# Strassen's seven products for the last 512 tokens of the second feed-forward layer, with its operand sums on GpSimd

## The chip, the cores and the metric

The kernel runs on one core of one Trainium2 chip. The time is the device time of one run in microseconds (us). The core has a matrix engine (TensorE, PE in the profile; PEld is its loading of weights), VectorE (DVE), ScalarE (ACT), GpSimd (POOL), and SyncE (SP), which issues the DMAs here. Each engine takes its instructions in program order and waits on semaphores for the others.

## The reference, cut to what matters

```python
x = attention(q, k, v)                     # 1536 tokens x 512
x = moe(x)                                 # first feed-forward layer, 512 -> 1024 -> 512
h = x @ w_in2                              # 512 -> 2048
g = np.where(h > 0, h, np.exp(np.minimum(h, 0)) - 1)
out = g @ w_out2                           # 2048 -> 512, the product that is changed for 512 of the 1536 tokens
```

Everything is in float32. A product of two float32 matrices is made here of three fast ones: each operand is split in a rounded part `hi` and the rest `lo`, and `mm3x` adds hi·hi, hi·lo and lo·hi in PSUM (lines 104 to 107).

## The kernel before

The 1536 tokens are three blocks of 512 (`TC`). The second layer has 16 slices of 128 features (`KF2`). Block 0 goes slice by slice. Blocks 1 and 2 make their first product `h` together, over eight pairs of slices (`NP3`, the loop over `p` at the end, 14.95 us a pair), with seven products of 512 columns in place of eight. In the same loop block 1's second product is done for the features that are ready (`fill`), and block 2's `g` is kept for later: `elu` makes g, splits it at once (ACT writes hi, DVE writes lo) into `g2[p]`. After the loop come two last fills of block 1, and then the **last stage**: block 2's second product, 16 slices x 4 token tiles x 3 matmuls = 192 matmuls of 512 columns, with g (128x128) as the weights and `w_out2`'s slice (512 columns) as the moving operand. The slices of `w_out2` lie split in DRAM (`w4d`) and are read back by `load_w4`, into three slots in turn (`w4r[n % 3]`) in the loop, and into larger space in the last stage.

PE's order in this part is the order of the code (`manual_schedule`). The order on ACT, DVE, POOL and SP is set by the scheduler, within the dependences; each engine then runs its list strictly in order. POOL has no work after 280 us. VectorE's instruction for lo is `lo_of` (line 102): a tensor_tensor that reads both inputs from SBUF.

Of the kernel before, what the change touches and what calls it, by code (L numbers as in the profile page):

```python
# [52 lines left out]
def tile_kernel(ctx: ExitStack, tc: tile.TileContext, qd, kT, v, w_in, w_out, g_ln, w_in2, w_out2,  # L53
                ident_d, mask_d, avg_d, out):
    nc = tc.nc
    scale = 1.0 / math.sqrt(D)
# [450 lines left out]
    for t, (j, n) in enumerate(ticks):  # L507
# [92 lines left out]
    def store(i, ops, t):  # L600
        o = rows[t]
        r0 = i * TC + t * 128
        if i == NTOK // TC - 1 and t == NTT - 1:
            for c in range(2):
                cs = slice(c * 256, (c + 1) * 256)
                if c:
                    nc.vector.tensor_copy(o[:, cs], ops[t][:, cs])
                else:
                    nc.scalar.activation(o[:, cs], ops[t][:, cs], AF.Copy)
                nc.sync.dma_start(out[r0:r0 + 128, cs], o[:, cs])  # L610
            return
# [54 lines left out]
    for p in range(NP3):  # L666
        w, c11, c12, c21 = w3_hl[p], *(psb.tile([128, TC], F32, tag="b", name=x) for x in ("c11", "c12", "c21"))
        s1, s2, s7, c22 = small
        product(c11, w["A11"], yf["B11"], True)
# [22 lines left out]
        if p + 2 < NP3:
            sums_w3(p + 2)
        if p:
            load_w4(KF2 + 2 * p + 1)
            if p + 1 == NP3:
                w4l_t = p_w3.tile([128, 6, 2, TC], F32R, tag="last", name="w4l")
                w4l[:] = [w4l_t[:, c] for c in range(6)]
                for n in range(2 * KF2, 2 * KF2 + 6):
                    load_w4(n)  # L700
# [5 lines left out]
        g2[p] = pool.tile([128, 2, 2, TC], F32R, tag=tag, name="g2", **({"bufs": 2} if p < 2 else {}))  # L706
# [71 lines left out]
```

## Time and profile before

| | us |
|---|---|
| median of 3 runs | 487.21 (486.96 to 487.42) |
| the profiled execution | 487.4 |
| its span, first to last instruction | 485.6 |
| PE busy | 460.9 (95%) |
| DVE, ACT, POOL busy | 331.9, 283.9, 127.4 |
| last stage (192 matmuls) | 437.98 to 481.50 |

The page divides the span in 40 slices of 12.1 us and gives the busy tenths of each engine. A timeline row gives start, duration, engine, line and operation, `out<-in` by the program's names, the shape, and in brackets the idle time ahead of it with what ended it. A matmul's shown duration holds its pipeline's latency, so the pace is read from start to start.

### The profile page before, as it was taken

To read this page: it belongs to the slowest core of one execution; us is meant where nothing else is said; L and a number is where in the kernel's file an instruction comes from. 1 tells how busy PE (TensorE), PEld (TensorE's weight loads), DVE (VectorE), ACT (ScalarE), POOL (GpSimd) and SP (SyncE) were. 2 spreads that over 40 slices of the span, in tenths; PEclk is the share of its full clock that TensorE was granted. 3 is DMA by queue.
4 is the path that set the end of the run, shared out by engine and by line. 5 is a ranking of instruction groups with operands and counts; after the bars stand their busy time and mean duration, and the time that the engine had idled before them with its cause. 6 is when DMAs were issued, how large, how long until landed. Compare 5 with 4: busy or idle time off the path is not lost.

```text
span 485.6 us, 7410 instructions
## 1 busy us (share of the span) xinstructions
PE 460.9 (95%) x2568; PEld 390.8 (80%) x2568; DVE 331.9 (68%) x747; ACT 283.9 (58%) x623; POOL 127.4 (26%) x200
## 2 busy tenths in 40 slices
PE   0989999899999999999999999999999999999996
PEld 0566787789997998899888888888888888888885
DVE  3698968997679377969997999557675565550000
ACT  1776777885658347655954757457676666660001
POOL 2798467476434222312232200000000000000000
PEclk9989999899999999999999999999999999999999
DMA  8993997254163413397579663651212212378112
GB/s 287 353 361 126 303 268 231 83 189 122 59 182 115 156 59 102 107 331 266 199 249 317 248 208 132 205 186 43 79 52 88 86 45 87 104 301 289 45 43 86
DMA packets 40117, 82.47 MB, mean 170 GB/s; under 512 B 9616, under 2 KB 18448, under 8 KB 40080
## 3 DMA queue, kind: packets, MB, share of 16 engines
q1 hardware_dynamic: 40080, 82.00, 51.0%
q8 instruction: 20, 0.33, 0.3%
q14 instruction: 17, 0.14, 0.1%
HBM read 70.46 MB, written 11.53 MB: 169 GB/s over the span
## 4 chain that ended last, share of the span: by engine, by line
PE 80%; DVE 12%; POOL 2%; issue 2%; ACT 2%; DMA 1%; SPq 0%; POOLq 0%; DVEq 0%
PE o_ps L107 9%; PE o_ps L105 9%; PE o_ps L106 9%; PE h L107 6%; PE h L105 6%; PE h L106 6%; PE c L107 5%; PE c L105 5%; PE c L106 5%; PE y_ps L105 4%; PE y_ps L107 4%; PE y_ps L106 4%; PE s_ps L216 3%; DVE conv L128 2%; DVE sm L222 2%
## 5 line engine op out<-in xcount | busy, mean ns | idle before, releaser
L126 POOL TENSOR_SCALAR conv<-conv 128x512 f32<-128x512 f32 x48 | 40.1, 838 | 91.1 <-ACT conv L123 87.1
L230 POOL TENSOR_SCALAR sm<-sm,st 128x120 f32<-128x120 f32 x96 | 49.4, 532 | 21.6 <-ACT ln L279 8.5
L105 PE MATMUL o_ps<-w4r,g_hl 128*128 128x512 f32 x128 | 49.8, 389 | 0.0
L106 PE MATMUL o_ps<-w4r,g_hl 128*128 128x512 f32 x128 | 49.8, 389 | 0.0
L107 PE MATMUL o_ps<-w4r,g_hl 128*128 128x512 f32 x128 | 45.3, 390 | 0.0
L105 PE MATMUL y_ps<-lnT,w_out 128*128 128x384 f32 x128 | 43.6, 341 | 1.0 <-DVE lnT L102 1.0
L105 PE MATMUL h<-w_in,xT 128*128 128x512 f32 x96 | 40.6, 423 | 3.3 <-ACT xT L136 3.3
L106 PE MATMUL y_ps<-lnT,w_out 128*128 128x384 f32 x128 | 43.2, 337 | 0.0
L107 PE MATMUL y_ps<-lnT,w_out 128*128 128x384 f32 x128 | 42.9, 337 | 0.0
L225 ACT ACTIVATE sm<-sm,st 128x120 f32<-128x120 f32 x96 | 36.8, 389 | 5.9 <-DVE st L222 5.9
L216 PE MATMUL s_ps<-kw,q_bd 128*128 128x120 f32 x192 | 28.5, 298 | 11.7 <-POOL kw L98 11.4
L107 PE MATMUL h<-w_in,xT 128*128 128x512 f32 x96 | 39.1, 407 | 0.2 <-DVE xT L102 0.2
L106 PE MATMUL h<-w_in,xT 128*128 128x512 f32 x96 | 38.7, 403 | 0.0
L216 PEld LDWEIGHTS s_ps<-kw,q_bd 128*128 128x128 f32 x192 | 26.8, 211 | 13.0 <-POOL kw L98 11.4
L613 DVE COPY y<-o_ps 128x512 f32<-128x512 f32 x5 | 3.5, 690 | 42.9 <-PE o_ps L107 42.9
L585 ACT ACTIVATE y<-y 128x512 f32<-128x512 f32 x48 | 30.0, 628 | 0.8
L127 DVE TENSOR_SCALAR conv<-conv 128x512 int32<-128x512 int32 x48 | 24.1, 503 | 8.7 <-POOL conv L126 8.7
L615 ACT ACTIVATE y<-o_ps 128x512 f32<-128x512 f32 x6 | 3.6, 599 | 43.9 <-PE o_ps L107 43.9
L106 PEld LDWEIGHTS o_ps<-w4r,g_hl 128*128 128x128 f32 x128 | 24.1, 188 | 5.1
L107 PEld LDWEIGHTS o_ps<-w4r,g_hl 128*128 128x128 f32 x128 | 23.9, 188 | 5.2 <-DVE g_hl L102 0.2
L105 PEld LDWEIGHTS o_ps<-w4r,g_hl 128*128 128x128 f32 x128 | 24.0, 188 | 4.9
L123 ACT ACTIVATE conv<-y 128x512 f32<-128x512 f32 x30 | 20.1, 671 | 13.5 <-DMA y<-in_w_in 11.9
(146 smaller groups left out, 1259.7 us busy)
## 6 DMA issues: line engine op xcount, KB each, us to landing
w4r<-w4d SPq DMA_DIRECT2D x38, 512.0 KB, 3.5
y<-in_w_in SPq DMA_DIRECT2D x16, 512.0 KB, 5.3
w4d<-w3f SPq DMA_DIRECT2D x16, 512.0 KB, 3.0
y<-in_w_out SPq DMA_DIRECT2D x14, 512.0 KB, 5.8
q_bd<-in_qd SPq DMA_DIRECT2D x24, 256.0 KB, 6.6
bits<-in_w_out SPq DMA_DIRECT2D x10, 512.0 KB, 4.8
w4l<-w4d SPq DMA_DIRECT2D x10, 512.0 KB, 4.2
vw<-in_v SPq DMA_DIRECT2D x24, 192.0 KB, 5.8
```

Of the source, the lines that this page charges most:

```text
L105: nc.tensor.matmul(ps, lhsT=l[0][ls], rhs=r[0][rs], start=first, stop=False, skip_group_check=parts)
L106: nc.tensor.matmul(ps, lhsT=l[0][ls], rhs=r[1][rs], start=False, stop=False, skip_group_check=parts)
L107: nc.tensor.matmul(ps, lhsT=l[1][ls], rhs=r[0][rs], start=False, stop=last, skip_group_check=parts)
L123: first = nc.scalar.activation(x, high.bitcast(F32), AF.Abs)
L126: nc.gpsimd.tensor_scalar(x, x, F64_HUGE, F64_TINY, op0=ALU.min, op1=ALU.max)
L127: nc.vector.tensor_scalar(a, a, 3, 0x3FFFFFF8, op0=ALU.logical_shift_left, op1=ALU.bitwise_and)
L128: nc.vector.scalar_tensor_tensor(a, high, -0x40000000, a, op0=ALU.bitwise_and, op1=ALU.bitwise_or)
L216: nc.tensor.matmul(sps[:, p, 0:KW], lhsT=q_bd[n][:, p, :], rhs=kw[:, p, :], start=True, stop=True)
L222: nc.vector.tensor_tensor_reduce(sm[:, p, :], sps[:, p, 0:KW], mask[:, mi, :], -scale, 3.0e38, op0=ALU.add, op1=ALU.min, accum_out=nm[:, p ...
L225: nc.scalar.activation(sm[:, p, :], sm[:, p, :], AF.Exp, bias=nm[:, p:p + 1], scale=-1.0, accum_out=ss[:, p:p + 1])
L230: nc.gpsimd.tensor_scalar(sm[:, p, :], sm[:, p, :], ri[:, p:p + 1], 1.0, op0=ALU.mult, op1=ALU.mult)
L585: nc.scalar.activation(m, m, AF.Exp, scale=-1.0)
```

## The change

**Second product of block 2.** For each pair `p` of slices, g is seen as 2x2 quarters (two slices by two halves of 256 tokens) and w_out2 as 2x2 quarters (two slices by two halves of 256 columns). `half` makes one of Strassen's seven products for it, of two token tiles with 256 columns: 6 matmuls, and so 8 x 7 x 6 = 336 matmuls of 256 columns in place of 192 of 512. The seven sums stay in seven PSUM banks over all pairs and are put together at the end, on DVE (`result`). Pairs 0 to 5 run pair by pair; the last two run product by product, so that the results come out one after the other.

**Operands.** Strassen's sums of w_out2's quarters (`sums_w4`, per pair two adds of 512 columns, which put hi and lo together again, and four of 256) and of g's quarters (`sums_g`, four of 256) are tensor_tensor instructions on POOL. `elu_m` now leaves g unsplit in `g2[p]`. `parts_g(p)` splits three pieces late, each with one copy on ACT and one `lo_of` on DVE: three quarters of g (768 columns), the sums of w_out2 (1024) and the sums of g (1024). `sums_g` of pairs 0, 1, 2, 4 and 6 write the same space in turn (`raw`), of pairs 3, 5 and 7 another. `load_b` brings the three quarters of w_out2 that are used as they are.

```diff
     def place_w4(n):
-        n -= 2 * KF2
-        return w4r[n % 3] if n < 0 else w4l[n % 6] if n < 10 else wt[:, (3, 4, 1, 2, 0, 3)[n - 10]]
+        return w4r[n % 3]
...
+    def elu_m(h2, m):
+        nc.scalar.activation(m, h2, AF.Relu, scale=-1.0)
+        nc.scalar.activation(m, m, AF.Exp, scale=-1.0)
+        nc.vector.scalar_tensor_tensor(m, m, -1.0, h2, op0=ALU.add, op1=ALU.max)
...
+    def add(out_, a, b, op=ALU.add):
+        nc.gpsimd.tensor_tensor(out_, a, b, op=op)
+
+    def sums_w4(p):
+        x = g2[0][:, 2048:3072].rearrange("p (c f) -> p c f", c=2)
+        t = g2[p][:, 1024:2048].rearrange("p (s f) -> p s f", s=4)
+        for c in range(2):
+            hi, lo = w4_hl[KF2 + 2 * p + c]
+            add(x[:, c], hi.bitcast(F32), lo.bitcast(F32))
...
+        add(t[:, 0], b12, b11, ALU.subtract)
+        add(t[:, 1], b22, t[:, 0], ALU.subtract)
+        add(t[:, 2], b22, b12, ALU.subtract)
+        add(t[:, 3], b21, t[:, 1], ALU.subtract)
...
+    def raw(p):
+        return g2[0 if p > 1 and p % 2 else 1][:, 2048:3072].rearrange("p (s f) -> p s f", s=4)
+
+    def sums_g(p):
...
+        add(sl[:, 0], a21, a22)
+        add(sl[:, 1], sl[:, 0], a11, ALU.subtract)
+        add(sl[:, 2], a11, a21, ALU.subtract)
+        add(sl[:, 3], a12, sl[:, 1], ALU.subtract)
+
+    def parts_g(p):
+        m = g2[p][:, 0:1024].rearrange("p (s f) -> p s f", s=4)
+        a, su, tu = last["a"][p % 3], unit(2 * p), unit(2 * p + 1)
+        for t, x in ((a, m[:, 0:3]), (tu, g2[p][:, 1024:2048].rearrange("p (s f) -> p s f", s=4)), (su, raw(p))):
+            first = nc.scalar.activation(t[:, 0], x, AF.Copy)
+            if p:
+                tc.keep_in_program_order(first)
+            lo_of(t[:, 1], x, t[:, 0])
+
+    def half(p, x, ps):
...
+        for t in range(2):
+            mm3x(ps[:, t], l, (al, slice(t * 128, (t + 1) * 128)), r, (al,), p == 0 and t == 0, p == NP3 - 1, True)
...
         for c, h2 in ((1, c22), (0, c12)):
-            ghl[2 * KF2 + 2 * p + c] = [g2[p][:, c, i] for i in range(2)]
-            elu(h2, ghl[2 * KF2 + 2 * p + c])
+            elu_m(h2, g2[p][:, (1 - c) * TC:(2 - c) * TC])
+        sums_w4(p)
...
-    ops = tiles_o()
-    for f in range(KF2):
-        for t in range(NTT):
-            ffn2_out(ops, t, 2 * KF2 + f)
-            if f == KF2 - 1:
-                store(2, ops, t)
-        if f != 9:
-            load_w4(2 * KF2 + f + 6 - (f > 9))
+    parts_g(1)
+    sums_g(2)
...
+    order = (1, 6, 7, 5, 2, 3, 4)
...
+    for p in range(NP3 - 2):
+        parts_g(p + 2)
+        if p + 3 < NP3:
+            sums_g(p + 3)
+        for x in order:
+            half(p, x, acc[x])
+        load_b(p + 3)
+    u1, u2, u3, u4 = tmp
+    for x in order:
+        for p in range(NP3 - 2, NP3):
+            half(p, x, acc[x])
+        if x == 1:
+            nc.scalar.activation(u1, acc[1], AF.Copy)
+        elif x == 6:
+            nc.vector.tensor_tensor(u2, acc[6], u1, op=ALU.add)
...
+        else:
+            result(4, u3, res[3], 1, 0)
```

How the change moves instructions is shown at three places. Brackets give what an instruction waits for; `Pool`, `DVE`, `Activation` and `PE` are the engines, `DMAHW` are DMAs.

GpSimd, the end of its list. Before, it ends with conversions of weights at 280 us:

```order
L126 TENSOR_SCALAR conv_85<-conv_85 128x512 [waits DVE_49,Activation_49]
L126 TENSOR_SCALAR conv_85<-conv_85 128x512 [waits Activation_49] x6
L126 TENSOR_SCALAR conv_85<-conv_85 128x512 [waits Activation_49]
L774 UNCONDITIONAL_BRANCH
L774 ISA [waits barrier_Pool_Activation_PE_DVE_SP_gather]
```

Now, around the start of the last stage (`g2_3298` is g2[0], `g2_3406` g2[1], `g2_3514` g2[2], `g2_3622` g2[3], `g2_3730` g2[4], `g2_4065` g2[7]):

```order
L648 TENSOR_TENSOR g2_3298<-w4r_2424 128x512 [waits DMAHW5_49]
L648 TENSOR_TENSOR g2_4065<-g2_3298,g2_4065 128x256 [waits Pool_49]
L648 TENSOR_TENSOR g2_4065<-g2_3298 128x256
L648 TENSOR_TENSOR g2_3298<-g2_3298,g2_3622 128x256 [waits Pool_49]
L648 TENSOR_TENSOR g2_3298<-g2_3622 128x256 [waits Pool_49]
L648 TENSOR_TENSOR g2_3298<-g2_3622,g2_3298 128x256 [waits Pool_49]
L648 TENSOR_TENSOR g2_3406<-g2_3514 128x256 [waits DVE_49]
L648 TENSOR_TENSOR g2_3406<-g2_3406,g2_3514 128x256 [waits Pool_49]
L648 TENSOR_TENSOR g2_3406<-g2_3514,g2_3406 128x256 [waits Pool_49]
L648 TENSOR_TENSOR g2_3406<-g2_3730 128x256 [waits DVE_49]
```

The rest of `sums_w4(7)` and of `sums_g(3)` stand ahead of `sums_g(2)` (the row `g2_3406<-g2_3514`), whose first add waits for DVE's last split of pair 1; `sums_g(4)` waits likewise for pair 2. Sixteen more adds follow `sums_g(2)`: pairs 4, 5, 6 and 7.

VectorE, the end of its list. Before, it has only the end of the loop and copies of results:

```order
L586 SCALAR_TENSOR_TENSOR y2_67<-y2_67,c12_3942 128x512 [waits Activation_49]
L102 TENSOR_TENSOR g_hl_2423<-y1_66,g_hl_2423 128x512 [waits Activation_49]
L102 TENSOR_TENSOR g2_4035<-y2_67,g2_4035 128x512 [waits Activation_49]
L613 COPY y0_65<-o_ps_3252 128x512 [waits DMAHW1_49,PE_49]
L613 COPY y0_65<-o_ps_3254 128x512 [waits DMAHW3_49,PE_49]
L613 COPY y0_65<-o_ps_4079 128x512 [waits DMAHW3_49,DVE_49,PE_49]
L607 COPY y0_65<-o_ps_4081 128x256 [waits DMAHW6_49,Activation_49]
```

Now (`s4` are slots for split sums):

```order
L606 COPY y0_65<-o_ps_3252 128x512 [waits DMAHW7_49,PE_49]
L606 COPY y0_65<-o_ps_3254 128x512 [waits DMAHW1_49,PE_49]
L102 TENSOR_TENSOR w4l_4017<-g2_3406,w4l_4017 128x768 [waits Activation_49]
L102 TENSOR_TENSOR s4_4025<-g2_3406,s4_4025 128x1024 [waits Activation_49]
L102 TENSOR_TENSOR s4_4024<-g2_3406,s4_4024 128x1024 [waits Activation_49]
L102 TENSOR_TENSOR w3e_3198<-g2_3514,w3e_3198 128x768 [waits Activation_49]
L102 TENSOR_TENSOR s4_4090<-g2_3514,s4_4090 128x1024 [waits Activation_49]
L102 TENSOR_TENSOR g_hl_2423<-g2_3406,g_hl_2423 128x1024 [waits Activation_49]
L102 TENSOR_TENSOR w3e_2096<-g2_3622,w3e_2096 128x768 [waits PE_49,Activation_49]
```

The splits of pairs 1 to 7, 21 `lo_of` in all, three a pair, stand behind the copies of block 1's last results (line 606).

ScalarE in the loop's first pair (`c11`, `c21` are products of pair 0). Before:

```order
L615 ACTIVATE y0_65<-o_ps_2572 128x512 [waits PE_49]
L615 ACTIVATE y0_65<-o_ps_2574 128x512 [waits PE_49]
L584 ACTIVATE y1_66<-c11_3199 128x512 [waits PE_49]
L585 ACTIVATE y1_66<-y1_66 128x512 [waits Activation_49]
L584 ACTIVATE y2_67<-y2_67 128x512 [waits DVE_49]
```

Now:

```order
L608 ACTIVATE y0_65<-o_ps_2572 128x512 [waits PE_49]
L608 ACTIVATE y0_65<-o_ps_2574 128x512 [waits PE_49]
L688 ACTIVATE w4r_2424<-g2_3298 128x1024 [waits Pool_49]
L581 ACTIVATE y1_66<-c11_3199 128x512 [waits PE_49]
L582 ACTIVATE y1_66<-y1_66 128x512 [waits Activation_49]
L581 ACTIVATE g2_3298<-y2_67 128x512 [waits DMAHW5_49,DVE_49]
```

The copy of pair 0's sums of w_out2 (`w4r_2424<-g2_3298`), which waits for POOL, has come in ahead of the elu of `c11`.

## Rows read from the trace of the kernel before

**Rows 1.** The page: busy time of each engine (share of the span) and its instructions.
```profile
PE 460.9 (95%) x2568; PEld 390.8 (80%) x2568; DVE 331.9 (68%) x747; ACT 283.9 (58%) x623; POOL 127.4 (26%) x200
```

**Rows 2.** Windows, last stage: busy of PE, PEld, DVE, ACT, POOL; clock; DMA share, GB/s.
```profile
437.98:481.50 43.52, 43.52 (x193) 35.86 (x191) 1.38 (x2) 1.13 (x3) 0.00 (x0) 1.00 0.30 100
```

**Rows 3.** Timeline, PE: first and last of 192 (512 columns) and of 12 (384).
```profile
437.98 0.39 PE L105 MATMUL o_ps<-w4l,g 128*128 128x512 f32 x1
481.29 0.39 PE L107 MATMUL o_ps<-w4r,g 128*128 128x512 f32 x1
...
212.00 0.33 PE L105 MATMUL y_ps<-lnT,w_out 128*128 128x384 f32 x1
213.91 0.33 PE L107 MATMUL y_ps<-lnT,w_out 128*128 128x384 f32 x1
```

**Rows 4.** Eight narrow matmuls in the chain of waits; their weight loads, by line.
```profile
120.36 0.88 PE s_ps L216 x8
...
L216 PEld LDWEIGHTS s_ps<-kw,q_bd 128*128 128x128 f32 x192 | 26.8, 211 | 13.0 <-POOL kw L98 11.4 <-DVE xT L102 0.7
```

**Rows 5.** Groups by line and shape: splits of 768 and 1024 columns (busy, mean ns).
```profile
L102 DVE TENSOR_TENSOR w3e<-w3f,w3e 128x768 fp32r<-128x768 f32 x8 | 7.7, 956 | 4.2 <-ACT w3e L136 3.3 <-PE o_ps L107 0.9
L102 DVE TENSOR_TENSOR w3l<-w3f,w3l 128x1024 fp32r<-128x1024 f32 x4 | 4.9, 1224 | 0.6 <-ACT w3l L136 0.5
L136 ACT ACTIVATE w3l<-w3f 128x1024 fp32r<-128x1024 f32 x4 | 4.2, 1046 | 0.0
```

**Rows 6.** GpSimd by line: shortest, median and longest ns of its instructions.
```profile
L98 POOL TENSOR_SCALAR kw<-k_sb x12: 510/513/947, 8.7 to 47.3; 128x384 f32<-128x384 f32 x12
L126 POOL TENSOR_SCALAR conv<-conv x48: 612/617/2578, 14.2 to 279.0; 128x512 f32<-128x512 f32 x48
L285 POOL TENSOR_TENSOR st<-st,negh x12: 544/554/1527, 57.0 to 202.5; 128x1 f32<-128x1 f32 x12
```

**Rows 7.** Timeline, two places where DVE and POOL run at the same time.
```profile
234.13 1.22 DVE L102 TENSOR_TENSOR w3l<-w3f,w3l 128x1024 fp32r<-128x1024 f32 x1
234.21 1.62 POOL L126 TENSOR_SCALAR conv<-conv 128x512 f32<-128x512 f32 x1 [2.21 <-ACT conv L123]
235.27 1.10 DVE L128 SCALAR_TENSOR_TENSOR conv<-bits,conv 128x512 int32<-128x512 int32 x1
...
221.13 0.95 DVE L102 TENSOR_TENSOR w3e<-w3f,w3e 128x768 fp32r<-128x768 f32 x1
221.15 2.01 POOL L126 TENSOR_SCALAR conv<-conv 128x512 f32<-128x512 f32 x1 [4.77 <-ACT conv L123]
222.00 0.69 DVE L128 SCALAR_TENSOR_TENSOR conv<-bits,conv 128x512 int32<-128x512 int32 x1
```

**Rows 8.** Timeline, end of the loop: last split for block 1, its reader, last copy.
```profile
434.63 0.68 DVE L102 TENSOR_TENSOR g_hl<-y,g_hl 128x512 fp32r<-128x512 f32 x1
435.48 0.39 PE L106 MATMUL o_ps<-w4r,g_hl 128*128 128x512 f32 x1
438.18 0.69 DVE L613 COPY y<-o_ps 128x512 f32<-128x512 f32 x1 [0.68 <-PE o_ps L107]
```

**Rows 9.** Timeline, pair 0: DVE's read of c12, and PE's next product into c12.
```profile
325.15 0.69 DVE L689 TENSOR_TENSOR y<-c,y 128x512 f32<-128x512 f32 x1 [2.03 <-PE c L107]
326.31 0.39 PE L105 MATMUL c<-yf,w3l 128*128 128x512 f32 x1
```

**Rows 10.** Timeline and windows: an idle PE and its granted clock (0.50 is 1.2 GHz).
```profile
92.12 0.65 PE L235 MATMUL p_ps<-ident,sm 128*120 128x128 f32 x2 [2.11 <-DVE st L222]
...
91.00:92.00 1.00, 0.00 (x0) 0.00 (x0) 1.00 (x6) 1.00 (x3) 0.04 (x2) 0.91 0.00 0
94.00:95.00 1.00, 1.00 (x6) 1.00 (x5) 0.58 (x3) 1.00 (x5) 1.00 (x3) 0.50 0.55 194
95.00:96.00 1.00, 1.00 (x8) 0.81 (x8) 1.00 (x9) 1.00 (x6) 0.60 (x2) 0.88 0.00 0
```

**Rows 11.** Timeline, after the last matmul: the last copy of a result.
```profile
482.13 0.42 DVE L607 COPY y<-o_ps 128x256 f32<-128x256 f32 x1 [1.08 <-ACT y L609]
```

More of the change, by code (lines that the diff above doesn't have):

```diff
@@ L395, in place_w4 @@
     def place_w4(n):
-        n -= 2 * KF2
-        return w4r[n % 3] if n < 0 else w4l[n % 6] if n < 10 else wt[:, (3, 4, 1, 2, 0, 3)[n - 10]]
+        return w4r[n % 3]
     def load_w4(n):
-        if n < 3 * KF2:
+        if n < 2 * KF2:
             t = place_w4(n)
@@ L583, in elu @@
         state["m"] += 1
-        nc.scalar.activation(m, h2, AF.Relu, scale=-1.0)
-        nc.scalar.activation(m, m, AF.Exp, scale=-1.0)
-        nc.vector.scalar_tensor_tensor(m, m, -1.0, h2, op0=ALU.add, op1=ALU.max)
+        elu_m(h2, m)
         split(*g, m)
@@ L602, in store @@
         r0 = i * TC + t * 128
[L603 to L611, printed above, removed]
         if t % 2:
@@ L651, in tile_kernel @@
     small = quarter[0][2:] + quarter[1][:2]
-    g2, w4l = {}, []
+    g2, last, units = {}, {}, {}
+    def add(out_, a, b, op=ALU.add):
[6 more added lines that the diff above has]
+            add(x[:, c], hi.bitcast(F32), lo.bitcast(F32))
+        (b11, b12), (b21, b22) = ([x[:, c, s * 256:(s + 1) * 256] for s in range(2)] for c in range(2))
+        add(t[:, 0], b12, b11, ALU.subtract)
+        add(t[:, 1], b22, t[:, 0], ALU.subtract)
+        add(t[:, 2], b22, b12, ALU.subtract)
+        add(t[:, 3], b21, t[:, 1], ALU.subtract)
@@ new lines, in unit, with load_b @@
+    def unit(u):
+        return units[u % 9].rearrange("p a b c -> p (a b c)").rearrange("p (c s f) -> p c s f", c=2, s=4)
+    def load_b(p):
+        if p < NP3:
+            t = last["b"][:, p % 3].bitcast(F32)
+            hl = [w4d[2 * p + c].rearrange("p (c s f) -> p c s f", c=2, s=2) for c in range(2)]
+            nc.sync.dma_start(t[:, :, 0], hl[0][:, :, 0])
+            nc.sync.dma_start(t[:, :, 1:3], hl[1])
+    def raw(p):
+        return g2[0 if p > 1 and p % 2 else 1][:, 2048:3072].rearrange("p (s f) -> p s f", s=4)
@@ new lines, in sums_g @@
+    def sums_g(p):
+        m = g2[p][:, 0:1024].rearrange("p (s f) -> p s f", s=4)
+        a12, a22, a11, a21 = (m[:, i] for i in range(4))
+        sl = raw(p)
+        add(sl[:, 0], a21, a22)
[3 more added lines that the diff above has]
+    def parts_g(p):
+        m = g2[p][:, 0:1024].rearrange("p (s f) -> p s f", s=4)
+        a, su, tu = last["a"][p % 3], unit(2 * p), unit(2 * p + 1)
[4 more added lines that the diff above has]
+            lo_of(t[:, 1], x, t[:, 0])
@@ new lines, in half @@
+    def half(p, x, ps):
+        side = lambda t, i: [t[:, c, i] for c in range(2)]
+        a, s_, t_, b = last["a"][p % 3], unit(2 * p), unit(2 * p + 1), last["b"][:, p % 3]
+        l, r = {1: ((a, 2), (b, 0)), 2: ((a, 0), (b, 1)), 3: ((s_, 3), (b, 2)), 4: ((a, 1), (t_, 3)),
+                5: ((s_, 0), (t_, 0)), 6: ((s_, 1), (t_, 1)), 7: ((s_, 2), (t_, 2))}[x]
+        l, r = side(*l), side(*r)
+        for t in range(2):
+            mm3x(ps[:, t], l, (al, slice(t * 128, (t + 1) * 128)), r, (al,), p == 0 and t == 0, p == NP3 - 1, True)
@@ L670, in tile_kernel @@
         nc.scalar.activation(s1, c11, AF.Copy)
+        if p + 1 == NP3:
+            units.update({0: w3l[0].rearrange("p a b c f -> p a b (c f)"), 1: wt[:, 3:5]})
+            last["a"] = [w3e[0].rearrange("p c s k f -> p c s (k f)")]
+            sums_g(0)
         product(c12, w["S2"], yf["T2"], True)
@@ L696, in tile_kernel @@
             if p + 1 == NP3:
[L697 to L700, printed above, removed]
+                last_t = p_w3.tile([128, 4, 2, 3, 256], F32R, tag="last", name="w4l")
+                last["b"] = last_t[:, 0:3]
+                last["a"] += [last_t[:, 3], w3e[1].rearrange("p c s k f -> p c s (k f)")]
+                for n in range(3):
+                    load_b(n)
+                units[2] = p_y.tile([128, 2, 2, TC], F32R, tag="yc", name="s4")
+                units[3] = p_y.tile([128, 2, 2, TC], F32R, tag="yd", name="s4")
+                parts_g(0)
+                sums_g(1)
             fill(KF2 + 2 * p - 1, ops)
@@ L715, in tile_kernel, with result @@
                 store(1, ops, t)
-    ops = tiles_o()
-    for f in range(KF2):
-        for t in range(NTT):
-            ffn2_out(ops, t, 2 * KF2 + f)
-            if f == KF2 - 1:
-                store(2, ops, t)
-        if f != 9:
-            load_w4(2 * KF2 + f + 6 - (f > 9))
+        if c == 0:
+            units[4] = w3l[1].rearrange("p c s k f -> p c s (k f)")
+            for u in range(2):
+                units[5 + u] = p_y.tile([128, 2, 2, TC], F32R, tag=f"y{u}", name="s4")
+    parts_g(1)
+    sums_g(2)
+    units[7], units[8] = gw[:, 0:2], gw[:, 2:4]
+    order = (1, 6, 7, 5, 2, 3, 4)
+    acc = {x: (psb if i < 4 else pso).tile([128, 2, 256], F32, tag="b" if i < 4 else "o", name="p_o")
+           for i, x in enumerate(order)}
+    tmp = [t.rearrange("p (t f) -> p t f", t=2) for t in quarter[0]]
+    res = [t.rearrange("p (t f) -> p t f", t=2) for t in rows]
+    def result(x, a, to, th, ch):
+        r0 = (NTOK // TC - 1) * TC + th * 256
+        for t in range(2):
+            nc.vector.tensor_tensor(to[:, t], acc[x][:, t], a[:, t], op=ALU.add)
+            nc.sync.dma_start(out[r0 + t * 128:r0 + (t + 1) * 128, ch * 256:(ch + 1) * 256], to[:, t])
+    for p in range(NP3 - 2):
[13 more added lines that the diff above has]
+            nc.vector.tensor_tensor(u2, acc[6], u1, op=ALU.add)
+        elif x == 7:
+            nc.vector.tensor_tensor(u3, acc[7], u2, op=ALU.add)
+        elif x == 5:
+            nc.vector.tensor_tensor(u4, acc[5], u2, op=ALU.add)
+            result(5, u3, res[0], 1, 1)
+        elif x == 2:
+            result(2, u1, res[1], 0, 0)
+        elif x == 3:
+            result(3, u4, res[2], 0, 1)
+        else:
+            result(4, u3, res[3], 1, 0)
     manual.__exit__(None, None, None)
```

2 lines of the change are left out of this document (1 added, 1 removed).

## The prediction

> **What bounds the kernel now.** The page first: PE is busy for 460.9 of 485.6 us, so a change pays only where it takes time out of PE, or costs where it makes PE wait [rows 1]. Then the stage that is changed, by the windows view: from 437.98 to 481.50 us PE is busy throughout at full clock, DVE and ACT do 1.4 and 1.1 us of work, POOL none [rows 2]. Before, the last stage waits for nothing: every operand was split earlier. It is 192 matmuls of 512 columns, from the first start to the last in 43.31 us, so 43.31/191 = 0.2268 us each [rows 3].
>
> **PE's work.** No matmul of 256 columns with split operands is in the trace, so its pace comes from two other widths. Twelve of 384 columns start 1.91 us apart, 0.1736 us each [rows 3]; from 384 to 512 columns the pace grows by 0.0532 us. A line through both gives 0.120 us at 256 columns (0.0133 us of it fixed). The change has 336 of them: 40.3 us against 43.5, **3.2 us less**, if PE never waits. A pair of slices takes 42 x 0.120 = 5.04 us.
>
> The weights could bound at this width, since each load shows 0.19 us or more. Eight matmuls of 120 columns took 0.88 us, 0.11 each, with loads of 0.211 us shown [rows 4]: loads overlap, and the line holds down to that pace. By the Trainium skill ("TensorE: Matmul & The Clock Gate", Part 2, LDWEIGHTS, and Part 3, The mechanism) a load takes 128/1.2 = 107 ns and overlaps a running matmul only when their row groups differ; an estimate by it is 0.107 + 0.107 us a matmul, 336 x 0.214 = 72 us, 28 more than before. The trace disagrees: between 384 and 512 columns only the columns' own time is added, and the 0.0133 us that stay are no 0.107.
>
> **What now has to keep up with PE.** The splits of block 2's g moved out of the loop, where DVE and ACT had room. In the last stage each pair needs three copies on ACT and three lo_of on DVE: one of 768 columns (0.956 us on DVE) and two of 1024 (1.224 each), 3.4 us a pair; on ACT 1.05 us for each 1024 [rows 5]. Taken alone both fit under 5.04 us a pair. POOL adds four tensor_tensor of 256 columns a pair.
>
> Their price first. The trace has no add of two tensors on POOL. Below: one-input instructions take 0.51 us for 384 columns and 0.612 for 512 [rows 6], so 0.20 + 0.0008 a column, 0.41 for 256. Two inputs one after the other through one path: 0.20 + 2 x 0.205 = 0.61. Above: the only two-input row takes 0.544 us for a single column [rows 6], plus 0.205 is 0.75. That row raises to a power, so I take **0.66**, nearer to 0.61. By the Trainium skill ("GPSIMD Engine Reference", section 3.1) an add over 2048 float32 columns took 4497 ns; scaled by columns that is an estimate of 0.56 us, which would make the total 487.6. No run here shows it yet.
>
> Now the point on which the forecast turns: **DVE and POOL exclude each other** when DVE reads two inputs from SBUF. At 234.13 DVE begins a lo_of of 1024 columns; POOL's instruction of 234.21, 0.612 us when alone, takes 1.62 and so ends at 235.83; it ran in the last 0.61 us, from 235.22, 0.13 ahead of the lo_of's end at 235.35. DVE's next, begun at 235.27, takes 1.10 us where the same line takes 0.69 in the second place, so it began in truth at 235.68, 0.15 before POOL's end [rows 7]. Each holds the path for its duration less about 0.14 us, and the other stands still. In the second place POOL, begun at 221.15, was even passed twice: through the lo_of at 221.13 and through the DVE instruction at 222.00 [rows 7]. All 21 late lo_of and all late adds are of these kinds.
>
> **The queue for that path.** DVE begins the splits of pair 1 when it has copied block 1's last result, at 438.9 [rows 8]. From there: 21 lo_of hold it 7 x (0.81 + 1.08 + 1.08) = 20.8 us. Sums_g of pairs 2, 4, 5, 6, 7 are 20 adds of 0.66 - 0.15 = 0.51 us: 10.2 us (pairs 0, 1, 3 come before). The path stands empty where one waits for the other. Sums_g(2) cannot begin before DVE's last split of pair 1, since both use the same space, and the last split of pair 2 waits for those adds and for ACT's copy of 1.05 us; with two handovers the path is empty for 1.3 us. The same happens at pair 7. About six adds follow the add they depend on with nothing of DVE between, 0.2 us each: 1.3 us. As DVE can pass POOL twice, I count one more such wait of 1.3 us, at pair 4 or 6 (none to three). Sum: 438.9 + 20.8 + 10.2 + 2.6 + 1.3 + 1.3 = 475.1 us for the last split of pair 7.
>
> PE wants it earlier. Six pairs take 30.2 us from 437.98; then product 1 of pairs 6 and 7 and product 6 of pair 6 take 2.16, so product 6 of pair 7 is due at 470.4. It starts some 4.5 us late (a small part of that already at pairs 2, 4 and at product 1 of pair 7). Two of its matmuls need no lo of this split, and eleven products of 0.72 us are left from it: 475.1 + 7.9 - 0.2 = 482.8. Before, the stage ended at 481.5: **1.3 us more**. What PE saves is eaten, and more, by the wait for the split.
>
> **Clock.** PE stands still for over 3 us in one place. Before 92.12 it had been idle for 2.1 us; in the last of these the granted clock was already falling (0.91), and it stayed at 0.50, 1.2 GHz, while PE worked, until it came back between 95 and 96 [rows 10]: low for 0.18 + 3 + 0.24 = 3.4 us by the means of the windows (0.91 and 0.88 at the ends). The same here costs up to half of that, 1.7 us, or nothing if it falls only while PE waits or not at all: I take **0.8**.
>
> **Upstream.** In the loop POOL's adds, 2 of 512 and 4 of 256 columns a pair, delay DVE by one add at a time, 1.1 us at most (0.20 + 2 x 0.42 and a margin). Nearly everywhere in the timeline PE reads DVE's results later than that. Two places have little room. Block 1's last lo ends at 435.31 and is read from 435.7 on (the third matmul, after the second at 435.48) [rows 8]; the rest of sums_w4(7) and sums_g(3) fall near there. In pair 0 ACT's copy of the w_out2 sums waits for POOL ahead of the elu of c11, and DVE's lo_of of it, 1.22 us, stands ahead of the read of c12 at 325.15 to 325.84, which PE awaits at 326.31 [rows 9]: 0.5 us of room. I take **0.3** for both, from 0 to 1.0. In return each pair loses two splits of 512 columns in the loop, which hide under PE: nothing. Load_b moves 0.75 MB a pair where 1 MB was moved, issued two pairs ahead: nothing.
>
> **Tail.** Before, after the last matmul came one copy on ACT and one on DVE of 0.42 us, one behind the other, each with its DMA [rows 11]; now two adds of 256 columns on DVE, each with its DMA: nothing.
>
> **Sum.** 1.3 + 0.8 + 0.3 = 2.4 us more. The profiled execution (487.4, of it 1.8 outside the span) would be 489.8; the median of the runs, 487.2, becomes **489.6**.
>
> **The rivals.**
> *The splits keep up* (0.25). If an add takes 0.5 us or less, or if the two engines alternate well, the queue is done before 470.4: at 0.41 an add holds the path 0.26 us, 5.2 in place of 10.2, and with no third wait it ends at 468.8. Then PE alone counts: 487.2 - 3.2 + 0.3 = 484.3, to 486.2 with a remaining wait of 2 us. It speaks for it that one-input work on POOL costs just that; against it, that an add reads twice as much.
> *Between* (0.15). Adds of 0.55 to 0.6 us and fair turns: a wait of 2 to 4 us at product 6 of pair 7 with the clock kept. 486.2 to 488.2, no difference that can be told.
> *The matmuls don't get shorter* (0.05). If the weight load as shown, 0.188 us, were the pace at 256 columns, 336 x 0.188 = 63.2 us, 19.7 more: 507. Rows 4 speak against it; so the change would not do what it says.
> *The forecast* (0.55): the wait for the path exceeds the saving, 488.2 to 492.5. The upper end is adds of 0.75 us (+1.8) with some of the clock's 0.9 and the upstream's 0.7 on top.
>
> **How the numbers follow.** Of slower by over 0.2% (1 us, about what a measurement of this kernel can tell from no change): 0.55 + 0.05 = 0.60; the same: 0.15; faster: 0.25. The likeliest case's own range is 488.2 to 492.5. To leave out no more than two in ten the range goes to the first rival's low end: 484.5 to 492.5.
>
> **What would show it.** Right: lo_of in the last stage lengthened beyond 1.22 us beside POOL, adds of 0.6 us and more, PE idle for about 3 us at the second product of pair 7 with DVE's last split ending near 475, a granted clock of 0.50 behind it. The pace of 256 columns at 0.120 us would show the saving real. Wrong: a PE without gaps from 438 to 478 (first rival), or adds under 0.5 us. A gap in pair 0 near 326 would show the upstream term too small.

## The result, and the profile after

The changed kernel takes 493.2 us (median of four runs, 491.2 to 494.2) against 487.3 for the kernel before on the same chip: **1.15% slower**, ratio 1.0115 [1.0077, 1.0152]. The forecast was slower at 489.6 with 492.5 as its upper end, so the sign was right and the time lies outside the range.

The profiled execution took 492.32 us, of it 490.5 in the span. The page of after, busy time of each engine and the chain that ended last (against [rows 1]), and behind them the same chain before:

```profile
PE 460.7 (94%) x2712; PEld 396.3 (81%) x2712; DVE 371.9 (76%) x764; ACT 295.4 (60%) x629; POOL 217.8 (44%) x280
...
PE 67%; DVE 12%; POOL 11%; ACT 4%; issue 2%; DMA 2%; SPq 1%; POOLq 0%; DVEq 0%
```

```profile
PE 80%; DVE 12%; POOL 2%; issue 2%; ACT 2%; DMA 1%; SPq 0%; POOLq 0%; DVEq 0%
```

PE's busy time is what it was (460.9 before), although 192 matmuls of 512 columns became 336 of 256: part of that work ran at half clock, as will be seen. In the chain PE fell from 80% to 67% and POOL rose from 2% to 11%; DVE's 12% are what they were.

The last stage of after in windows (busy of PE, PEld, DVE, ACT, POOL; clock; DMA share, GB/s), against [rows 2]:

```profile
438.67:449.00 10.33, 10.33 (x88) 10.33 (x87) 6.90 (x7) 5.54 (x8) 5.94 (x7) 1.00 0.56 190
449.00:474.00 25.00, 22.68 (x185) 22.00 (x184) 22.41 (x15) 12.66 (x15) 23.21 (x16) 1.00 0.36 117
474.00:481.00 7.00, 5.60 (x24) 5.30 (x25) 2.61 (x3) 1.37 (x2) 0.00 (x0) 0.51 0.00 0
481.00:486.19 5.19, 5.16 (x44) 4.95 (x42) 2.86 (x7) 0.00 (x0) 0.00 (x0) 1.00 0.32 108
```

Where PE alone was busy before, DVE and POOL are now both at about 90% from 449 to 474, and then follow seven microseconds at a clock of 0.51.

**The pace of a matmul** of 256 columns, timeline of PE in after, against [rows 3]:

```profile
438.67 0.28 PE L105 MATMUL p_o<-w4l,w3e 128*128 128x256 f32 x1
438.79 0.28 PE L106 MATMUL p_o<-w4l,w3e 128*128 128x256 f32 x1
438.90 0.28 PE L107 MATMUL p_o<-w4l,w3e 128*128 128x256 f32 x1
...
485.88 0.28 PE L107 MATMUL p_o<-s,w4l 128*128 128x256 f32 x1
```

They start 0.12 us apart, as the line through two wider matmuls said. Without a wait 335 steps would be 40.0 us (runs below); from first to last start there are 47.21.

**Who waits.** Timeline of PE in after, the starts behind a wait, each with the matmul ahead of it where the step is needed:

```profile
450.25 0.39 PE L107 MATMUL p_o<-s,g_hl 128*128 128x256 f32 x1 [0.45 <-DVE g_hl L102]
...
471.60 0.38 PE L107 MATMUL p_o<-w4l 128*128 128x256 f32 x1 [0.91 <-DVE w4l L102]
...
472.77 0.28 PE L107 MATMUL p_o<-g_hl,s 128*128 128x256 f32 x1
474.94 0.58 PE L105 MATMUL p_o<-s,s 128*128 128x256 f32 x1 [1.90 <-ACT s L688]
475.32 0.42 PE L106 MATMUL p_o<-s,s 128*128 128x256 f32 x1
476.20 0.58 PE L107 MATMUL p_o<-s,s 128*128 128x256 f32 x1 [0.46 <-DVE s L102]
```

From start to start these steps are longer than the pace by 0.60, 1.08 (the matmuls ahead start at 449.53 and 470.40), 2.05 and, from 474.94 to 476.20, by 1.02 us: **4.75 us** of waiting. The last two are product 6 of pair 7. The two chains behind it, DVE and POOL in after, and ACT's copy of that piece:

```profile
452.67 1.76 DVE L102 TENSOR_TENSOR s<-g,s 128x1024 fp32r<-128x1024 f32 x1
454.36 1.49 DVE L102 TENSOR_TENSOR w4l<-g,w4l 128x768 fp32r<-128x768 f32 x1
...
453.32 3.12 POOL L648 TENSOR_TENSOR g<-g,g 128x256 f32<-128x256 f32 x2
...
462.85 1.44 POOL L648 TENSOR_TENSOR g<-g 128x256 f32<-128x256 f32 x2
...
470.69 3.11 POOL L648 TENSOR_TENSOR g<-g,g 128x256 f32<-128x256 f32 x2
473.83 1.06 ACT L688 ACTIVATE s<-g 128x1024 fp32r<-128x1024 f32 x1 [3.68 <-POOL g L648]
474.92 1.23 DVE L102 TENSOR_TENSOR s<-g,s 128x1024 fp32r<-128x1024 f32 x1 [1.70 <-ACT s L688]
```

Beside each other, an add on POOL takes 1.55 us (two in 3.11) and a split of 1024 columns on DVE 1.76; where POOL is alone two adds take 1.44, and where DVE is alone the split takes 1.23 (the last row). So each split is 0.53 us longer, the time an add holds the path. The last split ends at 476.15, and 0.05 us later PE goes on.

**The clock** in after, windows of PE (busy, matmuls, clock, DMA share, GB/s):

```profile
474.00:475.00 1.00, 0.06 (x1) 0.54 0.00 0
475.00:480.00 5.00, 4.54 (x20) 0.50 0.00 0
480.00:481.00 1.00, 1.00 (x6) 0.55 0.00 0
```

It is at 0.50 (1.2 GHz) from about 474.1 to 480.9, 6.8 us. It fell while PE stood still, about 1.3 us behind the start of its last matmul at 472.77. From 476.20 to 481.00 PE makes 22 steps of 0.21 us and more in place of 0.12: 2.2 us.

So the profiled execution's 4.9 us more than before (492.3 against 487.4) are: the stage starts at 438.67 and not at 437.98, 0.69; from its first to its last matmul 47.21 and not 43.31, 3.90 (40.0, 4.75 of waits, 2.2 at half clock, 0.3 of longer steps next to the waits); from the last matmul's start to the end of the span 4.62 and not 4.31, 0.31.

### The profile page after: what moved, and what is told of

It reads as the page before. It is cut to its first block, busy times and chain, and to the rows that moved or that the text cites. A ratio compares the mean times of both kernels' runs of the same rounds, so it can differ in the third digit from the quotient of the medians.

```text
span 490.5 us, 7849 instructions
## 1 busy us (share of the span) xinstructions
PE 460.7 (94%) x2712; PEld 396.3 (81%) x2712; DVE 371.9 (76%) x764; ACT 295.4 (60%) x629; POOL 217.8 (44%) x280
## 4 chain that ended last, share of the span: by engine, by line
PE 67%; DVE 12%; POOL 11%; ACT 4%; issue 2%; DMA 2%; SPq 1%; POOLq 0%; DVEq 0%
POOL g L648 6%; PE h L107 6%; PE h L105 6%; PE h L106 6%; PE o_ps L107 6%; PE o_ps L106 6%; PE o_ps L105 6%; PE c L105 4%; PE c L107 4%; PE c L106 4%; PE y_ps L105 4%; PE y_ps L107 4%; PE y_ps L106 4%; POOL sm L230 3%; PE s_ps L216 2%
## 5 line engine op out<-in xcount | busy, mean ns | idle before, releaser
L126 POOL TENSOR_SCALAR conv<-conv 128x512 f32<-128x512 f32 x48 | 37.6, 784 | 93.2 <-ACT conv L123 88.6
L648 POOL TENSOR_TENSOR g<-w4r 128x512 f32<-128x512 f32 x16 | 21.3, 1330 | 90.7 <-DMA w4r<-w4d 89.7
L648 POOL TENSOR_TENSOR g<-g 128x256 f32<-128x256 f32 x36 | 43.4, 1219 | 9.5 <-DVE s L102 3.2
L102 DVE TENSOR_TENSOR g_hl<-y,g_hl 128x512 fp32r<-128x512 f32 x32 | 27.1, 848 | 7.5 <-ACT g_hl L136 7.4
L648 POOL TENSOR_TENSOR g<-g,g 128x256 f32<-128x256 f32 x28 | 30.1, 1076 | 1.0
```

The source lines that it names most:

```text
L126: nc.gpsimd.tensor_scalar(x, x, F64_HUGE, F64_TINY, op0=ALU.min, op1=ALU.max)
L648: nc.gpsimd.tensor_tensor(out_, a, b, op=op)
```

## Experiments

All were timed beside the kernel before; ratios with their 95% intervals. noadds, dvesums, late and warm share a chip and its runs of before (487.3 us), the two dve_ runs of 5 and 6, dve_loads and best another (487.9), the last four a third (488.0).

**1. The adds of g left out.** Is it POOL's adds, or are the late splits too slow by themselves?

```diff
     def sums_g(p):
         ...
+        if p > 1:
+            return
```

> The changed kernel without sums_g for pairs 2 to 7: the 24 adds of 256 columns that GpSimd makes of g in the last stage are left out, so the output is not the reference's; every split, matmul and DMA stays. Theory (the adds share a path with VectorE's lo_of, and that queue sets the end): without them 21 lo_of take about 21 x 1.14 = 24 us from 439, the last split is there long before it is due, PE never waits, the clock stays at full, and the last stage takes 336 x 0.120 = 40.3 us and some tenths: 484.6 to 486. Rival (the 21 late splits on VectorE and ScalarE are too slow by themselves, the adds do no harm): PE still waits at product 6 of pair 7, 490 or more.

Measured: 486.9 us, ratio 0.998 [0.997, 1.000]; the profiled execution 486.1. DVE's last splits of pair 7, and PE's last matmul:

```profile
466.19 2.36 DVE L102 TENSOR_TENSOR s<-g,s 128x1024 fp32r<-128x1024 f32 x2
...
479.22 0.28 PE L107 MATMUL p_o<-s,w4l 128*128 128x256 f32 x1
```

The splits are done at 468.6, each takes 1.22 again, PE waits for none of them, the clock stays at 1.00, and the stage takes 40.0 us. The rival falls. The median is 0.9 above the upper end expected. The profiled execution shows where time is lost outside the stage: pair 0 costs 1.2 us and the end behind the last matmul 5.1 in place of 4.3 (runs 5 and 6); the 0.8 from there to the median no profile shows.

**2. The same adds on DVE.** Is it the number of adds, or that another engine makes them? The other three adds of `sums_g` take `e` as well.

```diff
-        add(sl[:, 0], a21, a22)
+        e = nc.vector if p in (2, 4, 5, 6, 7) else None
+        add(sl[:, 0], a21, a22, ALU.add, e)
...
```

> The changed kernel with sums_g of pairs 2, 4, 5, 6 and 7 on VectorE in place of GpSimd: the same 20 adds, now in VectorE's own order, nothing on GpSimd beside them. Theory (two engines that exclude each other cost more than one that does both, since an add takes GpSimd 0.74 us and the handovers leave the path empty): lo_of 24 us and 20 adds of about 0.45 us, 9 us, from 439: last split of pair 7 at about 472 in place of 476.2, PE waits 1 to 2 us in place of 4, the clock may stay: 486.5 to 490. Rival (the queue's length is what counts, whoever makes the adds): the last split stays at 475 to 476, 492 to 494.

Measured: 486.5 us, ratio 0.998 [0.997, 0.999], 6.7 us below the changed kernel. DVE's groups from 440 us to the end of its splits, first of after and then of this run (busy, mean ns of one | idle ahead of them):

```profile
L102 DVE TENSOR_TENSOR s<-g,s 128x1024 fp32r<-128x1024 f32 x8 | 12.2, 1538 | 1.7 <-ACT s L688 1.7
```

```profile
L102 DVE TENSOR_TENSOR s<-g,s 128x1024 fp32r<-128x1024 f32 x8 | 9.6, 1216 | 0.0
L648 DVE TENSOR_TENSOR g<-g,g 128x256 f32<-128x256 f32 x10 | 4.1, 418 | 0.1
```

The splits are short again. Twenty adds, mostly 0.33 us from start to start, take DVE some 7 us, about what POOL's had cost it (thirteen splits longer by about 0.5 us each); but what it waited for ACT in after, 3.2, 1.7 and 1.7 us, is down to 1.1 and 0.3, since the adds no longer queue on POOL. DVE's last split ends at 471.6, 4.5 us earlier, as was expected; the 1 to 2 us of waiting that were expected with it did not come: the split is ready 0.25 us before PE takes it up (471.89). The clock stays at 1.00. So the adds as such are not the bound; making them on POOL beside DVE's splits is, where one takes 1.55 us. At the 0.72 us that POOL needs alone, twenty adds would be 14.4 us of a stage of 40; that POOL would then keep up is argued from this number and not run.

**3. A later due time, POOL as it was.** Pair 6 goes pair by pair as well, and pair 7's product 6 comes fourth.

```diff
-    order = (1, 6, 7, 5, 2, 3, 4)
+    order = (1, 2, 4, 6, 7, 5, 3)
...
-    for p in range(NP3 - 2):
+    for p in range(NP3 - 1):
```

> The changed kernel with pair 6 too gone through pair by pair, so that only pair 7 closes the seven sums, and the products in the order 1, 2, 4, 6, 7, 5, 3, which puts the product that needs the last split fourth: the split of pair 7 is then due at about 438.7 + 35.3 + 2.2 = 476.1 us and not at 471. All adds stay on GpSimd. Theory (the end is set by the last split against its due time): that split still ends at about 476, just when it is wanted, PE waits under 1 us, the clock stays at full: 485.5 to 488. Rival (GpSimd slows VectorE along the whole stage and each pair waits): the wait moves to pairs 4 to 6, 490 or more.

Measured: 488.6 us, ratio 1.004 [1.002, 1.006]. DVE's last split, PE's start on it, PE's last matmul and DVE's last adds:

```profile
475.72 1.23 DVE L102 TENSOR_TENSOR s<-g,s 128x1024 fp32r<-128x1024 f32 x1 [1.72 <-ACT s L688]
477.00 0.39 PE L107 MATMUL p_o<-s,s 128*128 128x256 f32 x1
...
479.61 0.28 PE L107 MATMUL p_o<-w4l,s 128*128 128x256 f32 x1
479.83 2.07 DVE L789 TENSOR_TENSOR y<-p_o,y 128x256 f32<-128x256 f32 x6
```

The split ends at 476.95, 0.8 us later than in after, and PE steps over it with 0.24 us lost: the stage takes 40.4 us. What was expected of the wait holds. The time missed its range by 0.6 for a reason that was not thought of: with all products closed one behind the other in 0.72 us, DVE comes to the results late, six adds stand behind the last matmul, and from its start to the end of the span it takes 6.4 us in place of 4.6.

**4. PE kept busy during the wait.** `keep_busy(n)` is n matmuls of 256 columns into a spare bank of PSUM. No operand comes earlier; only the clock can change.

```diff
+            if p == NP3 - 1 and x in (1, 6):
+                keep_busy(10 if x == 1 else 26)
             half(p, x, acc[x])
```

> The changed kernel with 36 matmuls of 256 columns more, whose results nobody reads: 10 in front of product 1 of pair 7 and 26 in front of its product 6, where PE waited 0.9 and 2.4 us. Theory (the lowered clock behind the wait costs about 2.4 us, in some runs more): PE does not stand still, the granted clock stays at full to the end, and the time falls from 493.2 to 490 to 491, with less spread from run to run; the wait for the split itself stays, so it is not below 489. Rival (the clock falls for another cause than the wait, or costs nothing): 493 or, with the matmuls added, up to 494.

> The changed kernel once more, beside the next run on one chip. Theory (the clock that falls behind the wait costs 2 to 3 us and differs from run to run): 492 to 494 with granted clocks from 0.983 to 0.993, and the low runs slow. Rival (the first runs were unlucky): 490 or less.

> The run warm (36 matmuls more, that nobody reads, in front of products 1 and 6 of pair 7) once more, beside the run after_again on one chip. Theory (a lowered clock behind the wait, 2.4 us): 1.5 to 2.5 us below after_again, the intervals of the two ratios apart. Rival (the clock's share is small, and the 0.7% found for warm was the chip's): within 0.5 us of after_again.

Measured: 491.5 us, ratio 1.0085 [1.0060, 1.0109], beside the changed kernel's 1.0115 in its own runs; then, both on one chip, 491.9 and 1.0068 [1.0045, 1.0091] against 493.7 and 1.0104 [1.0078, 1.0131]. In the profiled executions the clock, first in after_again, then in warm:

```profile
473.00:474.00 1.00, 0.00 (x0) 0.70 0.00 0
474.00:480.00 6.00, 5.31 (x23) 0.50 0.00 0
480.00:481.00 1.00, 1.00 (x9) 0.88 0.00 0
```

```profile
470.00:474.00 4.00, 4.00 (x36) 1.00 0.00 0
474.00:478.00 4.00, 4.00 (x36) 1.00 0.00 0
478.00:482.00 4.00, 4.00 (x36) 1.00 0.02 4
```

With PE busy the clock stays at full, and the stage takes 45.4 us in place of 47.2, in the second pair 44.9 in place of 46.9: 1.8 and 2.0 less. The medians fall by 1.7 and 1.8; the first, 491.5, is 0.5 above what was expected. The intervals of the two ratios overlap a little in either pair; but of ten runs of each kernel, six of the changed kernel's are longer than the longest with the added matmuls (492.4), and the medians differ the same way in both pairs. The clock of the changed kernel also tells its runs apart: 491.2 and 491.3 us at a mean of 0.993, 491.8 and 492.3 at 0.990, 493.4 to 495.2 at 0.984 to 0.986. With the matmuls added there is no such order: 490.5 us at 0.993, 492.4 at 0.997. So executions of one kernel also differ by about 2 us for a reason that is not the clock, and that no profile here shows.

**5. and 6. What is left ahead of the stage and behind it**, on the kernel of run 2. First, pair 0's split of the w_out2 sums is moved to pair 3 of the loop (`part_t`: the copy on ACT, held in program order, and the lo_of on DVE):

```diff
+        if p == 3:
+            units[1] = wt[:, 3:5]
+            part_t(0, True)
```

> The kernel of the run dvesums (late adds of g on VectorE), and in it the split of pair 0's w_out2 sums moved from pair 0 of the loop, where ScalarE's copy of it waited for GpSimd and VectorE's lo_of of it stood in front of the read of c12, to pair 3. Theory (that split delays the elu of pair 0, and TensorE waited 0.3 to 0.8 us at 331 us for it in every trace of a changed kernel): the wait at 331 us is gone, 0.3 to 0.8 us less than dvesums: 485.7 to 486.2. Rival (the one-input of the delay is GpSimd's adds beside VectorE, whatever the split): the wait stays, 486.5.

Then, apart from that, the last product in two banks:

```diff
+    acc4b = pso.tile([128, 2, 256], F32, tag="o", name="p_o")
+    at = lambda x, t: acc4b[:, 0] if x == 4 and t else acc[x][:, t]
```

> The kernel of the run dvesums, and in it the last product, 4, summed in two banks of PSUM, so that the result of its first 128 tokens can be added while the second 128 are still computed. Theory (behind the last matmul stand two adds of 0.38 us on VectorE and two DMAs one after the other, where before a copy of 0.38 and one of 0.42 us on two engines did): one add and one DMA go ahead of the last matmul, 0.3 to 0.6 us less than dvesums: 485.9 to 486.2. Rival (the last DMA's own time sets the end): no change.

Measured: 486.0 us, 0.9959 [0.9946, 0.9972], and 485.9 us, 0.9957 [0.9942, 0.9972], as expected; but run 2 had 0.998 [0.997, 0.999] on another chip, and the intervals overlap a little. The wait at 331 us, as in after, and behind it the row that made it:

```profile
324.34 1.23 DVE L102 TENSOR_TENSOR w4r<-g,w4r 128x1024 fp32r<-128x1024 f32 x1 [1.31 <-ACT w4r L688]
325.48 0.68 DVE L741 TENSOR_TENSOR y<-c,y 128x512 f32<-128x512 f32 x1
...
330.92 0.50 PE L105 MATMUL c<-yf,w3e 128*128 128x512 f32 x1 [0.29 <-DVE y L583]
```

All of after's 0.69 us ahead of the stage lie there: steps too long by 0.11, 0.45 and 0.11 us from 326 to 331, none after that. With the split moved the profile names no wait there, and 0.4 us of longer steps remain. Behind the last matmul, DVE in dve_tail:

```profile
480.16 0.78 DVE L792 TENSOR_TENSOR y<-p_o,y 128x256 f32<-128x256 f32 x2 [0.31 <-PE p_o L107]
480.19 0.28 PE L107 MATMUL p_o<-s,w4l 128*128 128x256 f32 x1
```

The first of the two adds starts with the last matmul, and the end comes 4.2 us after that matmul's start where it was 4.7 in run 2.

**7. All together, and more.** The loads of the last stage behind the last `w4r` load and pair 3's adds on DVE as well (dve_loads), and this with runs 5 and 6 and another order of the products (best). Both hold the first add of each pair in the program's order on DVE:

```diff
-        add(sl[:, 0], a21, a22, ALU.add, e)
+        first = add(sl[:, 0], a21, a22, ALU.add, e)
+        if p > 1:
+            tc.keep_in_program_order(first)
```

> The kernel of the run dvesums, and in it the load of block 2's last w_out2 slices issued ahead of the first three loads of the last stage in place of behind them, and pair 3's sums of g moved to VectorE too. Theory (in dvesums TensorE waits 0.5 us at 437 us because GpSimd's add of those slices, 435.12 to 436.41, runs beside block 1's last lo_of, which takes 1.66 us in place of 0.69; the slices came late because 2.25 MB stood ahead of them): the adds are done before 435, the lo_of takes 0.69, the wait is gone; four more adds of 0.37 us on VectorE may make product 6 of pair 7 wait up to 1 us: 485.6 to 487. Rival (the load was not late for that reason): GpSimd's adds stay at 435, 486.5 and more.

> All of these together: late adds of g on VectorE, pair 0's split at pair 3, the loads in the other order, the last product in two banks; and product 2 put second and product 6 third, which makes the last split of pair 7 due 1.4 us later and so covers the four more adds on VectorE. Theory (the costs found are separate and add up): TensorE without a wait from 325 us to the end, 484.4 to 485.4, 0.4 to 0.6% less than the kernel before. Rival (they hide one another, or the last adds of VectorE come late): 486 to 486.5.

Measured: 493.7 us, 1.0115 [1.0097, 1.0132], and 489.8 us, 1.0044 [1.0025, 1.0063]. Both expectations failed. In dve_loads, POOL's add of the last slices, and DVE's splits of the sums of pairs 5, 6 and 7:

```profile
429.28 1.31 POOL L648 TENSOR_TENSOR g<-w4r 128x512 f32<-128x512 f32 x1 [3.26 <-DMA w4r<-w4d]
...
465.19 1.23 DVE L102 TENSOR_TENSOR w4r<-g,w4r 128x1024 fp32r<-128x1024 f32 x1 [1.13 <-ACT w4r L693]
...
470.89 1.23 DVE L102 TENSOR_TENSOR s<-g,s 128x1024 fp32r<-128x1024 f32 x1 [1.13 <-ACT s L693]
...
474.71 0.42 DVE L648 TENSOR_TENSOR g<-g,g 128x256 f32<-128x256 f32 x1
476.25 1.23 DVE L102 TENSOR_TENSOR s<-g,s 128x1024 fp32r<-128x1024 f32 x1 [1.12 <-ACT s L693]
```

The add did move from 435 to 429, and the wait at 437 us is gone. But with its adds held in place DVE makes the last add of a pair, waits 1.1 us for ACT's copy of that sum, and only then splits it, since nothing else stands between. These splits come 5.7 us apart, where a pair takes PE 5.0: pair by pair DVE falls behind, PE waits 3.9 us in the stage by the profile, and the clock falls again. In run 2 the scheduler had put splits of other pieces there. POOL has no adds of g beside these splits, so it is the same stall, a queue that ends late, from another cause. In best the same wait of 1.1 us stands ahead of each such split, and the stage takes 44.5 us with the clock at 1.00. That the hold is the cause is read from these rows: no run has it alone, and pair 3's four adds are on DVE in both. Whether the new load order alone gains is left open too, since it ran only with the adds held in place.

**8. The two edits that helped**, on run 2, with run 2 beside it:

> The run dvesums once more, as the base for the next. Theory: 0.998 of the kernel before, as measured. Rival (that number was the chip's, since dve_tu0 and dve_tail stood at 0.996 on another): 0.996, and then neither of the two edits brought what their 0.9 us seemed to show.

> The run dvesums with both edits that helped: pair 0's split of the w_out2 sums moved to pair 3, and the last product in two banks of PSUM. Theory (0.3 to 0.8 us at 331 us and 0.4 us behind the last matmul, apart from each other): 0.7 to 1.2 us below dvesums_again, 0.994 to 0.996 of the kernel before. Rival (the wait at 331 us comes back at 437 us, where block 1's last lo_of runs beside GpSimd): only the 0.4 us of the tail.

Measured: 486.4 us, 0.9969 [0.9953, 0.9985], and **485.2 us, 0.9941 [0.9924, 0.9957]**. 1.3 us for both together, a little over what was expected; the intervals overlap a little. This version is 0.6% faster than the kernel before and 1.7% faster than the changed one. Run 2's 0.997 lies between the two values that were weighed, so part of the gain seen in 5 and 6 may be the chip's.

The profiled executions differ in three places: pair 0 costs 0.5 us and not 0.8, the end behind the last matmul 4.35 and not 4.7, and the 0.7 us that PE loses at 436 us in run 2, where block 1's last lo_of runs beside POOL's add of the last slices, are not lost. (That the two stand only 0.3 us apart, 485.3 and 485.0, comes from the time ahead of the loop, which has the same code and took 1.1 us more in the second.) The third belongs to neither edit. POOL's add waits for a DMA: in run 2 it takes 434.44 to 435.74, and the lo_of begun at 434.72 takes 1.57 us; here it ends at 435.55, and the lo_of begun at 435.48 takes 0.68. Two executions of one kernel differ in it as well (none in after, 0.3 us in after_again). So how much of the 1.3 us the two edits brought stays open.

The first and last matmul of the stage:

```profile
438.82 0.28 PE L105 MATMUL p_o<-w4l,w3e 128*128 128x256 f32 x1
...
478.82 0.28 PE L107 MATMUL p_o<-s,w4l 128*128 128x256 f32 x1
```

40.0 us: PE's whole saving is there, 3.3 us against [rows 3].

## Why the prediction was right and wrong

- **PE's work, −3.2 us:** right. 40.0 us where 40.3 was said; weight loads don't bound at 256 columns. (The fixed part of that line is 0.014 us by its own two widths and not 0.0133; nothing hangs on it.) The 72 us worked out from the Trainium skill's rule on row groups don't fit steps of 0.12 us; the same page ("TensorE: Matmul & The Clock Gate", Part 2, Step-by-step) also lets a load go ahead into a background buffer of weights, which does.
- **The price of an add, 0.66 us:** within its bounds. Alone it is 0.72 (two in 1.44), nearer to the upper bound of 0.75 than to the value taken. By the Trainium skill ("GPSIMD Engine Reference", section 3.1) 0.56 had been estimated; the trace has more.
- **DVE and POOL exclude each other:** right, shown by after's rows (0.53 us longer a split, where 0.51 was taken as an add's hold) and by runs 1 and 2, where both lengthening and wait are gone.
- **The queue:** right. 36.2 us were said from block 1's last copy to the end of pair 7's last split; it took 36.6 (439.56 to 476.15). The two handovers said, at pairs 2 and 7, are in DVE's timeline as waits for ACT of 3.2 and 1.7 us. The third, put at pair 4 or 6, came at pair 5 with 1.7, and the path was not empty in it: POOL made two adds there (462.85). The parts fit less closely than the sum, so that it fits within 0.4 us is partly luck.
- **The due time and the wait, 4.5 us in all:** right. It was 4.75, most of it where it was said: 3.07 at product 6 of pair 7, in two parts, 1.08 at product 1 of pair 7 and 0.60 at pair 2. With the 0.3 us of longer steps next to the waits, the stage without the clock would be 1.7 us longer than before; 1.3 was said.
- **The clock, 0.8 us, at most 1.7: this step failed.** That the clock falls in the wait was right; its price was not. The low stretch was taken from the one in [rows 10], 3.4 us long. Here it was 6.8 us and reached 4.7 us past the end of the wait: 2.2 us, and run 4 gives 1.8 and 2.0 back by keeping PE busy and nothing else. The 0.8 was the middle of two guesses, and its upper bound half of one stretch in one execution. That stretch too had followed a wait of 2.1 us, with PE busy behind it. In after the same wait leaves the clock at full (timeline of PE, and a window with its busy time, matmuls and clock):

```profile
92.37 0.62 PE L235 MATMUL p_ps<-ident,sm 128*120 128x128 f32 x4 [2.10 <-DVE st L222]
...
92.00:95.00 3.00, 2.63 (x19) 1.00 0.55 174
```

So a wait of about 2 us was followed by nothing, 3.4 or 6.8 us of low clock, and the size of the wait alone does not give the price. What makes it the longer one here (the wait of 1.08 us shortly before, the second part of 1.02 behind it) no run separates.
- **Upstream, 0.3 us:** 0.69 in the profile of after, inside its 0 to 1.0, and all of it in pair 0, the second of the two places named; the other, block 1's last lo, costs nothing in after, 0.3 us in after_again, and a wait of 0.5 and 0.6 us in runs 2 and 3, where its lo_of takes 1.66 and 1.78 us beside POOL's add (run 8 shows what decides it).
- **Tail, nothing:** 0.3 us. Two adds on one engine in a row are longer than a copy on each of two.

The sum for the profiled execution was 489.8 and it is 492.3: 1.4 of the difference is the clock, 0.4 upstream, 0.3 the tail, 0.4 the stage's waits. That execution still lies inside the range; the median, 0.9 above it, does not, and the forecast had no term for how executions differ. The mean clocks of the changed kernel's runs (0.984 to 0.993) speak for the clock as part of the 0.9. They do not prove it: the mean is over the whole span, where the stretch at 92 us is low in one execution and not in another, and with PE kept busy in the stage the median still lies 0.7 and 0.9 us above the profiled executions. Where those 0.9 us arise stays open. The rival "the splits keep up" is what runs 1 and 2 show once POOL has no adds.

## What to carry to other kernels

Work that moves to an idle engine is not free when it shares a path with the engine that is waited for: price the pair as one queue, in the stage where it runs, against the time its last result is due. When the sum of such a queue says that TensorE will stand still, add the clock on the far side of the wait, and with room above the longest stretch that one trace shows: here it was twice that, and cost nearly half as much as the wait itself. And an instruction held in program order to fix one stall can take away the work that hid another: look at what stands between an add and the split that needs ACT's copy of it.

## What the runs showed of the hardware

- Two tensor_tensor of 256 columns on GpSimd took 1.44 us alone and 3.1 us beside VectorE's splits; on VectorE the same add is shown with 0.42 us and the next starts 0.33 us later.
- The granted clock stayed at 0.50 for 6.8 us, from within a standstill of 2.05 us, although TensorE worked without a gap from 476.20 on. In dve_loads it fell for 6.8 us (476.1 to 482.9) in a step too long by 1.6 us, with one of 1.4 three microseconds before; in the run best, steps too long by 0.5 to 1.4 us, in four places, left the clock at 1.00 in the profiled execution.
- The standstill of 2.1 us at 92 us left the clock at 0.50 behind it in the profiled executions of before and dvesums and at 1.00 in those of after, noadds and warm, and in dvesums_again, which is the kernel of dvesums.
- The mean clock of the changed kernel differed between runs from 0.984 to 0.993, and the time with it; with TensorE kept busy the ten runs had 0.991 to 0.997, and their times, 489.7 to 492.4, did not follow it.
